# A long-convolution kernel with generated taps: decay tables laid out four channels wide, the input spectrum formed unfolded on TensorE, a new load order, evacuations on either engine

## The chip, the cores and the metric

One core of one Trainium2 chip. The metric is the device time of the whole kernel in microseconds (us), the median of four runs of each kernel. Each run also has a span (first to last instruction in the trace) and a mean granted TensorE clock; the time is about 2 us longer than the span. A run is called "fast" unless it is over 1.5% above the fastest of the same kernel. Engines: PE is TensorE, PEld its weight loads, DVE is VectorE, ACT is ScalarE, SP issues transfers.

## The reference, cut to what matters

```python
# x: [1, 2048, 512] bf16
dt = exp(log_dt); logdA = dt * (A_re + i A_im); dB = dt * (B_re + i B_im)
P  = exp(logdA[:, :, None] * l[None, None, :])          # 512 channels x 128 states x 2048 lags
K  = einsum("dn,dnl,dn->dl", C, P, dB).real             # the taps of a long convolution
y  = irfft(rfft(pad(u)) * rfft(pad(K)))[:, :, :L] + u * Dskip
# besides: a router picks 2 of 2048 rows, a small FFN (512 -> 1792 -> 512) updates them,
# and the result is g * y + (1 - g) * b, with g = sigmoid((x * gate_w).sum(-1))
```

The kernel never forms `P`. A lag is split into a sum of one of 32 coarse offsets and one of 21 others; each factor is a complex exponential, built in a table on ACT (exponentials and sines) and DVE (complex products). (The 32 x 21 = 672 sums are enough because the reference rounds the lags to bf16, so far fewer than 2048 of them differ.) Matmuls multiply the two tables over the 128 states and so form all taps: **tap generation**. One pair of matmuls (real and imaginary part) does a group of four channels, so a half takes 64 x 2 = 128; each multiplies 4 x 32 weights by 4 x 21 = 84 columns, and only the blocks in which both channels are the same are used. The 512 channels are done as two halves, "half 0" and "half 1". The convolution runs in the frequency domain with DFT matrices: **forward** (spectrum of the input), **kernel spectrum**, products on DVE, **inverse**. Each of these has two output blocks of 1024 steps.

## The kernel before: the parts that matter

Tables are stored one offset after another, each with its 256 channels in a row. Tap generation takes channels `g`, `g` + 64, `g` + 128 and `g` + 192 together, so both of its operands are strided. The weights (`TP`) lie 64 x 2 bytes = 128 bytes from element to element; in the moving operand (`TQ`) it is 256 x 2 = 512 bytes from one offset to the next.

```python
# tap generation: 128 matmuls of 84 columns for each half
for g in range(b0, b0 + ng):
    for part in range(2):
        last = hh.matmul(pb(0, 128, (g - b0) * 84, (1, 84)),
                         TP[h](0, 128, part * 32 * HC + g, (64, 128)),              # weights
                         TQ[h](0, 128, part * NJ * HC + g, (64, 4), (HC, NJ)),      # moving
                         start=(part == 0), stop=(part == 1))
# ... cut ...
# forward: even and odd steps apart (144 matmuls of 512 columns), ACT evacuates, DVE adds and subtracts
AC(ev(0, 128, 0, (1, 1024)), pb(0, 128, 0, (1, 1024)), ACTF.Copy, [pb.buf], [ev])
for pm in range(2):
    TT(o, i0, i1, SUB if pm else ADD, [ev], [...])
# ... cut ...
# the order of the work as it is handed to a list scheduler: exps1/tab1 and exps2/tab2 are exponentials and products
# of the two tables, xupd the update of rows by the FFN, kgen tap generation, kspec the kernel spectrum
exps1(0, 0); tab1(0, 1, False); routing(); forward()
exps2(0, 2); tab2(0, 3, False); exps1(1, 4); xupd(); tab1(1, 5, True); kgen(0)
exps2(1, 6); tab2(1, 7, True); kspec(0); kgen(1)
products(0, 0); products(0, 1); kspec(1); inverse(0); products(1, 0); products(1, 1); inverse(1)
```

All loads are issued by SP on one queue. A scheduler in the program places each operation by estimated costs when the kernel is built; on the chip every engine runs its list in that order and waits on semaphores.

## Time and profile before

| | before |
|---|---|
| time, median (range) | 292.08 us (291.55 to 294.74) |
| span of the profiled run | 291.4 us |
| PE, DVE, ACT busy | 191.5, 194.2, 143.4 us |
| tables done, first product may start (T) | 201.2 us |
| from T to the end | 90.2 us |

The first part of the page (busy time, share of the span, instruction count) and two rows of its second part (tenths in 40 slices of 7.3 us; PEclk is the granted clock):

```profile
PE 191.5 (66%) x1298; PEld 126.6 (43%) x1298; DVE 194.2 (67%) x347; ACT 143.4 (49%) x252; POOL 0.2 (0%) x4
...
DVE  0001796699799998110059619999991099999993
...
PEclk9999956959758655575555555589855579997999
```

No engine is full. DVE has three holes: before 27 us, near 130 to 148 us, and at 220 to 233 us. The groups (operation, count, busy us, mean ns, idle time before and what ended it):

```profile
L694 PE MATMUL ps<-AR 128*128 128x84 bf16 x256 | 47.9, 371 | 14.9 <-DVE AR L374 14.9
L694 PEld LDWEIGHTS ps<-AR 128*128 128x128 bf16 x256 | 45.0, 180 | 17.6 <-DVE AR L374 15.0
...
L735 PEld LDWEIGHTS ps<-AR 128*128 128x128 bf16 x224 | 22.0, 101 | 12.9 <-issue 2.9
```

L694 is tap generation. Its weight loads take 180 ns against 101 ns for a contiguous 128 x 128 load. The mean of one matmul there (371 ns) is a latency; what counts is how many finish in a stretch. The timeline of PE (start, us, operation, count, idle time before) gives that, and the timeline of DVE gives the holes:

```profile
108.99 13.43 PE L694 MATMUL ps<-AR 128*128 128x84 bf16 x72 [14.94 <-DVE AR L374]
...
205.80 23.73 PE L694 MATMUL ps<-AR 128*128 128x84 bf16 x128
229.35 2.65 PE L735 MATMUL ps<-AR 128*128 128x256 bf16 x8
```

```profile
27.18 0.69 DVE L374 TENSOR_TENSOR AR<-AR 128x512 f32<-128x512 bf16 x1 [27.18 <-ACT AR L385]
...
148.57 0.43 DVE L378 TENSOR_SCALAR AR<-AR 128x1024 bf16<-128x1024 bf16 x1 [19.41 <-ACT AR L385]
...
233.17 30.25 DVE L374 TENSOR_TENSOR AR<-AR 128x2048 bf16<-128x2048 bf16 x33 [13.23 <-ACT AR L385]
```

From the first start of the 128 tap matmuls to the start of the next matmul it is 229.35 - 205.80 = 23.55 us, 184 ns each. All rates below are taken in this way, as the duration of a row holds its last matmul's latency too. (The prediction names T as 200.6 and has 186 ns; the last table operation begins at 200.5 and ends at 201.2.) The hole of 13.23 us at 220 to 233 stands behind that stretch: the kernel spectrum that the products need is queued on PE after it.

### The profile page before, as it was taken

The page shows a single profiled execution, that of the slowest core. Times are in us where ns is not written, and L with a number is a line of the kernel's source. Part 1 is how long each engine was busy: PE and PEld are TensorE (multiplying, and loading weights), DVE is VectorE, ACT ScalarE, POOL GpSimd, SP SyncE. Part 2 cuts the span into 40 slices and gives each one's busy share as a digit, 9 for nine tenths or more (in the row PEclk, how much of TensorE's full clock was granted, in tenths as well). Part 3 has the DMA queues.
Part 4 walks back from the last instruction along what each step waited for, and adds up shares of the span by engine and source line. Part 5 has one row for each costly group of instructions (what it writes and reads, how often), then busy time and mean ns, then how long its engine had stood idle before and what let it go on. Part 6 is the DMA issues. An engine that isn't in the chain of part 4 may idle for free.

```text
span 291.4 us, 3307 instructions
## 1 busy us (share of the span) xinstructions
PE 191.5 (66%) x1298; PEld 126.6 (43%) x1298; DVE 194.2 (67%) x347; ACT 143.4 (49%) x252; POOL 0.2 (0%) x4
## 2 busy tenths in 40 slices
PE   0089109839319009999820250999999989977994
PEld 0035003513304009758310100266899666665883
DVE  0001796699799998110059619999991099999993
ACT  1023058997992402425999989855422335410000
POOL 0000000000000000000000000000000000000000
PEclk9999956959758655575555555589855579997999
DMA  7998690000160000000740000000000340002213
GB/s 283 351 207 127 183 369 1 3 0 0 43 208 2 0 0 1 2 0 0 291 213 0 3 0 0 0 0 2 0 0 2 103 184 2 1 0 74 58 52 108
DMA packets 21793, 20.97 MB, mean 72 GB/s; under 512 B 13073, under 2 KB 19346, under 8 KB 21394
## 3 DMA queue, kind: packets, MB, share of 16 engines
q1 hardware_dynamic: 21778, 20.76, 23.1%
q8 instruction: 10, 0.16, 0.2%
q14 instruction: 5, 0.04, 0.0%
HBM read 15.78 MB, written 2.10 MB: 61 GB/s over the span
## 4 chain that ended last, share of the span: by engine, by line
DVE 38%; PE 32%; ACT 16%; SPq 9%; issue 3%; DMA 1%; DVEq 0%
DVE AR L374 29%; PE ps L694 15%; ACT AR L385 14%; PE ps L735 6%; DVE AR L381 6%; SPq L448 6%; DVE AR L378 3%; PE ps L785 2%; PE ps L652 2%; PE ps L669 2%; PE ps L803 2%; PE ps L802 2%; ACT L231 2%; SPq L388 1%; DMA AR<-in_A_B_re_dram 1%
## 5 line engine op out<-in xcount | busy, mean ns | idle before, releaser
L374 DVE TENSOR_TENSOR AR<-AR 128x1024 bf16<-128x1024 bf16 (+6 forms) x222 | 146.6, 728 | 59.5 <-ACT AR L385 56.0
L385 ACT ACTIVATE AR<-AR 128x256 bf16<-128x256 f32 (+5 forms) x164 | 75.1, 542 | 31.7 <-DVE AR L374 11.5
L385 ACT ACTIVATE AR<-ps 128x1024 bf16<-128x1024 f32 (+6 forms) x64 | 50.7, 806 | 78.3 <-PE ps L694 31.0
L669 PE MATMUL ps<-AR 128*128 128x512 bf16 x128 | 37.9, 443 | 31.2 <-ACT AR L385 17.1
L694 PE MATMUL ps<-AR 128*128 128x84 bf16 x256 | 47.9, 371 | 14.9 <-DVE AR L374 14.9
L694 PEld LDWEIGHTS ps<-AR 128*128 128x128 bf16 x256 | 45.0, 180 | 17.6 <-DVE AR L374 15.0
L669 PEld LDWEIGHTS ps<-AR 128*128 128x128 bf16 x128 | 13.8, 112 | 50.5 <-ACT AR L385 18.4
L735 PE MATMUL ps<-AR 128*128 128x256 bf16 x224 | 34.0, 289 | 0.7 <-ACT AR L385 0.7
L785 PE MATMUL ps<-AR 128*128 128x256 bf16 x256 | 30.2, 281 | 4.4 <-DVE AR L381 4.4
L785 PEld LDWEIGHTS ps<-AR 128*128 128x128 bf16 x256 | 25.5, 101 | 8.8 <-DVE AR L381 5.0
L735 PEld LDWEIGHTS ps<-AR 128*128 128x128 bf16 x224 | 22.0, 101 | 12.9 <-issue 2.9
L378 DVE TENSOR_SCALAR AR<-AR 128x256 int32<-128x256 f32 (+5 forms) x48 | 12.7, 327 | 21.8 <-ACT AR L385 21.6
L381 DVE SCALAR_TENSOR_TENSOR AR<-AR 128x1024 int16<-128x1024 int16 (+2 forms) x20 | 22.8, 1148 | 0.1
L802 PE MATMUL ps<-AR 128*128 128x512 bf16 x16 | 9.3, 578 | 17.1 <-ACT AR L385 17.1
L707 PE MATMUL ps<-AR 128*32 128x128 bf16 (+1 forms) x96 | 8.6, 379 | 13.2 <-ACT AR L385 13.2
L381 DVE SCALAR_TENSOR_TENSOR AR<-ps,AR 128x256 bf16<-128x256 f32 x32 | 13.1, 475 | 2.4 <-PE ps L785 2.4
L802 PEld LDWEIGHTS ps<-AR 128*128 128x128 bf16 x16 | 1.7, 105 | 22.5 <-ACT AR L385 20.5
L385 ACT ACTIVATE AR<-ps,AR 128x512 bf16<-128x512 f32 x16 | 10.2, 682 | 1.8 <-PE ps L803 1.8
L707 PEld LDWEIGHTS ps<-AR 128*32 128x32 bf16 x96 | 3.9, 122 | 16.3 <-ACT AR L385 14.6
L803 PE MATMUL ps<-AR 2*128 2x512 bf16 x16 | 9.2, 575 | 0.0
L599 PE MATMUL ps<-AR 128*128 128x128 f32 x4 | 1.5, 374 | 10.8 <-DVE AR L378 10.8
L672 PE MATMUL ps<-AR 128*128 128x512 bf16 x16 | 7.1, 443 | 0.0
(29 smaller groups left out, 48.2 us busy)
## 6 DMA issues: line engine op xcount, KB each, us to landing
AR<-c_ksp SPq DMA_DIRECT2D x1, 3584.0 KB, 11.1
AR<-c_fwd SPq DMA_DIRECT2D x1, 2048.0 KB, 7.6
AR<-in_A_u_dram SPq DMA_DIRECT2D x2, 1024.0 KB, 11.0
AR<-c_inv SPq DMA_DIRECT2D x1, 2048.0 KB, 7.8
out_dram<-AR SPq DMA_DIRECT2D x16, 128.0 KB, 2.2
AR<-in_B_w_gate_dram SPq DMA_DIRECT2D x1, 1792.0 KB, 7.3
AR<-in_B_w_up_dram SPq DMA_DIRECT2D x1, 1792.0 KB, 11.3
AR<-in_B_w_down_dram SPq DMA_DIRECT2D x1, 1792.0 KB, 7.4
```

Source lines behind the costliest of these rows:

```text
L374: return P.op(DVE, lambda h: h.tensor_tensor(out=o, in0=a, in1=b, op=op), rd, wr, cost=tt_cost(o, a, b), **k)
L378: return P.op(DVE, lambda h: h.tensor_scalar(out=o, in0=a, scalar1=s1, scalar2=None, op0=op0), rd, wr, cost=c, **k)
L381: return P.op(DVE, lambda h: h.scalar_tensor_tensor(out=o, in0=a, scalar=sc, in1=b, op0=op0, op1=op1), rd, wr, cost=0.16 + nel(o) * 1.04e- ...
L385: return P.op(ACT, lambda h: h.activation(out=o, in_=a, func=func, scale=scale, bias=bias), rd, wr, cost=0.185 + nel(o) * 0.833e-3 + (0.09 ...
L448: P.op(SP, lambda h, db=db: h.dma_start_transpose(XT(0, 128, db * L, (1, L)), dr(A_u, db * 128, (D, L), (1, 128))), [], [(XT, db)], cost=0 ...
L669: last = h.matmul(pb(0, 128, par * 512, (1, 512)), F(0, 128, ((par * 4 + st) * 2 + part) * 512 + ft * 128, (1, 128)), U(0, 128, (blk * 8 + ...
L694: last = hh.matmul(pb(0, 128, (g - b0) * 84, (1, 84)), TP[h](0, 128, part * 32 * HC + g, (64, 128)), TQ[h](0, 128, part * NJ * HC + g, (64 ...
L707: last = hh.matmul(pb(32 * g, 32, c4 * 64, (256, njg), (1, 64)), lw, KA[h](0, 128, c4 * NJ + 8 * bk + g, (4, njg), (84, 64)), start=True, ...
L735: last = hh.matmul(pb(0, 128, n * 256, (1, 256)), KP(0, np_, u * 2048 + tau * 128, (1, 128)), KC[h](0, np_, jg * 256, (1, 256)), start=(k ...
L785: last = hh.matmul(pb(0, 128, e * 256, (1, 256)), G(0, 128, ((par * 2 + part) * 4 + ft) * 512 + (2 * t2 + e) * 128, (1, 128)), X(0, 128, h ...
L802: h.matmul(pb(0, 128, c0, (1, D)), IDN(0, (1, 128)), U(0, 128, tb * D, (1, D)), start=True, stop=False)
L803: return h.matmul(pb(0, 128, c0, (1, D)), OHR(0, 2, tb * 128, (1, 128)), ZB(0, 2, D, (1, D)), start=False, stop=True)
```

## The change

The intent: make both operands of tap generation contiguous, take additions from DVE, start the tables earlier, and let evacuations go to whichever of ACT and DVE the scheduler finds free first. Tables get the layout (64 groups of channels) x (offset) x (4 channels), so for one group the 128 weights lie in a row, and so do the 84 moving columns. ACT and DVE then write and read in runs of four bf16 values.

```diff
-   TP[h](0, 128, part * 32 * HC + g, (64, 128)),  TQ[h](0, 128, part * NJ * HC + g, (64, 4), (HC, NJ))
+   TP[h][1 - part](0, 128, g * 128, (1, 128)),    TQ[h][1 - part](0, 128, g * 84, (1, 84))
 # exponentials, an example
-   AC(TP[h](0, 128, 32 * HC + s * HC, (1, HC)), AL(0, 128, h * HC, (1, HC)), ACTF.Exp, ...)
+   AC(TP[h][1](0, 128, s * 4, (128, 64), (1, 4)), AL(0, 128, h * HC, (4, 64), (1, 4)), ACTF.Exp, ...)
 # cosine: an addition to the integer argument in place of an absolute value
-   STT(hv(1), hv(0), -1.0, hv(0), ALU.mult, ALU.max, ks, [(a, "abs")])
+   TS(w, w, 16384.0, ALU.add, ks, ks)
 # forward: sum and difference formed in PSUM, with a negated matrix: 272 matmuls, no DVE additions
-   AC(ev(...), pb(...), ACTF.Copy, [pb.buf], [ev]);  TT(o, i0, i1, SUB if pm else ADD, [ev], ...)
+   w = ng(...) if par and pm else F(...);  EV(X(...), pb(...), [pb.buf], ...)
 # copies out of PSUM and scalings: either engine, chosen when the schedule is made
+   def EV(o, a, rd, wr, **k): return P.op((ACT, DVE), (activation Copy, tensor_copy), rd, wr, ...)
 # loads: decay parameters first on SP; input U, DFT matrix F and small constants on ACT's queue
-   for i in range(6): P.op(SP, ... dma_start_transpose(PRM ...) ...)
+   for i in (1, 0, 2, 3, 4, 5): P.op(SP, ... dma_start_transpose(PRM ...), prio=...)
+   DMA([(U ...)], ..., eng=ACT, prio=2e5);  DMA([(F ...)], ..., eng=ACT, prio=1.9e5)
 # the last stage of half 0: ACT scales the inverse into YA, DVE adds it (16 updates leave DVE)
+   AC(YA(...), pb(...), ACTF.Copy, ..., scale=SG(...));  TT(u, u, YA(...), ADD, ...)
 # order
-   exps1(0, 0); tab1(0, 1, False); routing(); forward(); exps2(0, 2); tab2(0, 3, False); ...
+   exps1(0, 0); exps2(0, 0); routing()  # boosted;  tab1(0, (1, 1)); forward(); tab2(0, (1, 3)); ...
```

The diff also regroups ACT's loads of function tables (8 loads of 1.28 us in the trace of before) and changes some of the scheduler's estimated costs.

## The prediction

> **What bounds it now.** Span 291.4 us. Busy line: DVE 194 us, PE 192, ACT 143; none is full. Chain of waits: DVE 38%, PE 32%, ACT 16%. Stretches, by the timeline:
> 1. DVE starts at 27 us: the parameter transposes are issued behind the input, its transposes and the DFT matrix.
> 2. Tables of half 0 on DVE, to 120.
> 3. First tap generation (L694): 72 matmuls in 13.4 us, 186 ns each. DVE idles 129 to 148 us, waiting for ACT's exponentials (19.4 in the waits).
> 4. Tables of half 1, to T = 200.6 us.
> 5. Products and inverse, T to the end: 91 us, of which DVE waits 13.2 us (220 to 233) for the kernel spectrum stuck behind the second tap generation (128 matmuls, 23.7 us).
>
> **What the change does.**
> - Tap weights are contiguous. Their loads now take 180 ns (groups by form). Contiguous loads with 2-column matmuls ran 64 in 1.74 us, 27 ns each; 84 columns warm are about 35 ns (512 took 215). Estimate: 50 to 90 ns per matmul, 128 in 8 to 11 us instead of 23.7. The Trainium skill (SBUF — State Buffer, 16-byte cachelines) says that each access crossing to a new line pays; weights 128 bytes apart do. Runs of four bf16 should keep DVE's rate (1024 elements 0.70 us); that is my main doubt.
> - Forward: 32 DVE adds of 0.43 us vanish (-13.8), but PE goes from 144 to 272 matmuls of 512 columns: 58 us warm (215 ns), against 31. Cold they take 427 ns (both rates are in this trace).
> - 16 absolute values (1.38 us each) become integer adds (about 0.7, from 0.43 for 512 fp32 elements): -11 us DVE. Some scalings and 16 output updates leave DVE; a few evacuations join. DVE total about 165 us; ACT about 155; PE 170 to 190.
> - DMA: decay parameters first on one queue, input and matrix on the other. ACT starts its 48 exponentials (0.32 us each) near 8 us, DVE tables near 26, without the pause of stretch 3.
> - In the instruction order, routing and its FFN now precede the forward transform on PE. Weights land about 33 us; I expect the forward to start at 40 to 46 us instead of 14.
>
> **Critical path after.** Forward plus first tap generation occupy PE about 75 us (58 + 10 + cold start and some FFN), to 116 to 121. The second half's exponentials reuse memory of the negated matrices and wait for it, about 9 us of ACT, then tab2 of half 1, about 33 us on DVE: T = 155 to 162. After T, 91 - 13.2 = 78 us remain, since tap generation now hides behind the first products (15 us). Sum: 235 us. The PE doubling is on the path and eats part of the gain.
>
> **Predicted: 235 us**, 8 in 10 between 218 and 252. Faster over 2%: 0.97; within 2%: 0.02; slower: 0.01.
>
> **What would show it.** L713 at 90 ns or less per matmul; DVE busy 160 to 172; DVE tables starting before 30 us; forward starting at 40 to 46; T near 158; no wait over 3 us between T and the last products; 1024-element DVE products still 0.70 us.
>
> **What would make it wrong.** Four-wide runs slow DVE or ACT (1.2 us per 1024-element product would add about 40 us); in-order EV copies on DVE or ACT stall tables behind a late forward (slower); routing finishing early or evacuations overlapping better, T near 140 (faster, about 218).

## The result, and the profile after

| | before | after |
|---|---|---|
| time, median (range) | 292.08 (291.55 to 294.74) | 246.94 (244.86 to 248.39) us |
| ratio | 1 | 0.843, 95% interval 0.835 to 0.852 |
| PE, DVE, ACT busy | 191.5, 194.2, 143.4 | 172.5, 170.4, 146.9 us |
| T | 201.2 | 162.7 us |
| from T to the end | 90.2 | 82.0 us |

A ratio here is the mean time of one kernel's fast runs over the mean of the other's fast runs in the same rounds, so it is not quite the ratio of the medians quoted beside it.

The change is 45 us faster, within the predicted range, and 12 us short of the number predicted. The same rows of the page and the same groups as before:

```profile
PE 172.5 (70%) x1426; PEld 103.4 (42%) x1426; DVE 170.4 (70%) x279; ACT 146.9 (60%) x278; POOL 0.2 (0%) x4
...
DVE  0002223899995039989850299969999999999872
...
PEclk9999999999999999999999755589997999996798
...
L713 PE MATMUL ps<-AR 128*128 128x84 bf16 x256 | 11.8, 201 | 2.4 <-ACT AR L402 2.4
L713 PEld LDWEIGHTS ps<-AR 128*128 128x128 bf16 x256 | 10.6, 98 | 4.5 <-ACT AR L402 3.2
```

Weight loads of tap generation went from 180 to 98 ns. The timeline of PE shows the first tap matmuls, the start of the forward and the end of the kernel:

```profile
59.33 10.18 PE L693 MATMUL ps<-AR 128*128 128x512 bf16 x40
...
111.41 1.07 PE L713 MATMUL ps<-AR 128*128 128x84 bf16 x24
112.31 3.61 PE L693 MATMUL ps<-AR 128*128 128x512 bf16 x16
...
204.59 14.15 PE L804 MATMUL ps<-AR 128*128 128x256 bf16 x128
224.27 16.64 PE L804 MATMUL ps<-AR 128*128 128x256 bf16 x128 [5.53 <-ACT AR L398]
```

24 tap matmuls took 112.31 - 111.41 = 0.90 us from the first start to the next matmul's, 37.5 ns each, about a fifth of before. But the forward (L693) began at 59.3 us, and 128 inverse matmuls (L804) start only when the last product of block 1 is done (224.8 us); they run on for 11.2 us after the last product of all (229.7). The start of the kernel, on the timelines of DVE and ACT, and the landing times of transfers (last number, us from issue):

```profile
22.62 0.69 DVE L387 TENSOR_TENSOR AR<-AR 128x512 f32<-128x512 bf16 x1 [10.30 <-DMA AR<-in_A_A_im_dram]
...
41.28 0.69 DVE L391 TENSOR_SCALAR AR<-AR 128x1024 int32<-128x1024 int32 x1 [3.62 <-ACT AR L398]
...
89.59 1.23 DVE L402 CAST AR<-ps 128x1024 bf16<-128x1024 f32 x1 [12.81 <-PE ps L695]
```

```profile
24.99 0.72 ACT L406 ACTIVATE AR<-AR 128x256 int32<-128x256 f32 x2 [10.70 <-DVE AR L387]
...
26.54 12.34 ACT L398 ACTIVATE AR<-AR 128x256 bf16<-128x256 f32 x40
```

```profile
AR<-in_A_A_re_dram SPq DMA_TRANSPOSE x1, 10.3
AR<-in_A_A_im_dram SPq DMA_TRANSPOSE x1, 19.4
```

The two decay parameters were issued first, yet `A_im` landed 19.4 us after its issue; before, its transpose took 3.9 us. `A_im` is needed for the argument scalings (L406), which ACT has in its list ahead of 40 of the exponentials. Those exponentials need only `A_re`, but ACT runs its list in order and the scalings stand first, so they ran at 26.5 to 38.9 us and the tables on DVE started at 41.3.

### The profile page after: what moved, and what is told of

Its sections match the earlier page's. It is cut to its first block, busy times and chain, and to the rows that moved or that the text cites. A ratio compares the mean times of both kernels' runs of the same rounds, so it can differ in the third digit from the quotient of the medians.

```text
span 244.7 us, 3534 instructions
## 1 busy us (share of the span) xinstructions
PE 172.5 (70%) x1426; PEld 103.4 (42%) x1426; DVE 170.4 (70%) x279; ACT 146.9 (60%) x278; POOL 0.2 (0%) x4
## 4 chain that ended last, share of the span: by engine, by line
PE 43%; DVE 24%; ACT 20%; DMA 8%; issue 3%; SPq 1%; DVEq 0%; ACTq 0%
DVE AR L387 21%; PE ps L693 19%; ACT AR L398 13%; DMA AR<-in_A_A_im_dram 8%; PE ps L804 7%; PE ps L754 6%; ACT AR L402 3%; PE ps L831 3%; PE ps L830 2%; ACT AR L406 2%; DVE AR L391 2%; PE ps L659 1%; PE ps L670 1%; PE ps L695 1%; ACT L242 1%
## 5 line engine op out<-in xcount | busy, mean ns | idle before, releaser
L387 DVE TENSOR_TENSOR AR<-AR 128x1024 bf16<-128x1024 bf16 (+5 forms) x182 | 136.8, 804 | 34.7 <-DMA AR<-in_A_A_re_dram 11.6
L398 ACT ACTIVATE AR<-AR 128x256 bf16<-128x256 f32 (+2 forms) x132 | 64.7, 560 | 15.4 <-DVE AR L391 4.8
L402 ACT ACTIVATE AR<-ps 128x1024 bf16<-128x1024 f32 (+6 forms) x58 | 45.5, 806 | 30.7 <-PE ps L754 17.7
L693 PE MATMUL ps<-AR 128*128 128x512 bf16 x256 | 59.6, 385 | 0.0
L693 PEld LDWEIGHTS ps<-AR 128*128 128x128 bf16 x256 | 25.1, 99 | 30.5 <-issue 1.9
L804 PE MATMUL ps<-AR 128*128 128x256 bf16 x256 | 30.8, 286 | 5.5 <-ACT AR L398 5.5
L804 PEld LDWEIGHTS ps<-AR 128*128 128x128 bf16 x256 | 26.1, 103 | 10.0 <-DVE AR L387 5.8
L754 PEld LDWEIGHTS ps<-AR 128*128 128x128 bf16 x224 | 21.9, 101 | 12.2 <-issue 1.5
L398 ACT ACTIVATE AR<-ps,AR 128x512 bf16<-128x512 f32 (+1 forms) x32 | 16.6, 586 | 15.5 <-DVE AR L387 10.4
L598 PE MATMUL ps<-AR 128*128 128x2 bf16 x64 | 1.8, 165 | 32.2 <-DMA AR<-in_A_u_dram 32.2
L406 ACT ACTIVATE AR<-AR 128x256 int32<-128x256 f32 x50 | 17.6, 405 | 10.9 <-DVE AR L387 10.7
L391 DVE TENSOR_SCALAR AR<-AR 128x1024 int32<-128x1024 int32 (+5 forms) x32 | 16.2, 524 | 8.4 <-ACT AR L398 8.0
L402 DVE CAST AR<-ps 128x1024 bf16<-128x1024 f32 (+3 forms) x6 | 5.1, 865 | 22.5 <-PE ps L695 15.4
L830 PE MATMUL ps<-AR 128*128 128x512 bf16 x16 | 8.1, 509 | 11.0 <-ACT AR L398 11.0
L598 PEld LDWEIGHTS ps<-AR 128*128 128x128 bf16 x64 | 1.8, 104 | 32.1 <-issue 32.1
L713 PE MATMUL ps<-AR 128*128 128x84 bf16 x256 | 11.8, 201 | 2.4 <-ACT AR L402 2.4
L713 PEld LDWEIGHTS ps<-AR 128*128 128x128 bf16 x256 | 10.6, 98 | 4.5 <-ACT AR L402 3.2
L617 PE MATMUL ps<-AR 128*128 128x128 f32 x4 | 1.9, 475 | 12.8 <-DVE AR L391 12.8
L394 DVE SCALAR_TENSOR_TENSOR AR<-ps,AR 128x256 bf16<-128x256 f32 x16 | 6.9, 479 | 4.1 <-PE ps L804 4.1
L830 PEld LDWEIGHTS ps<-AR 128*128 128x128 bf16 x16 | 1.6, 100 | 15.7 <-ACT AR L398 14.6
## 6 DMA issues: line engine op xcount, KB each, us to landing
AR<-in_B_w_up_dram SPq DMA_DIRECT2D x1, 1792.0 KB, 11.2
```

Of the source, the lines that this page charges most:

```text
L387: return P.op(DVE, lambda h: h.tensor_tensor(out=o, in0=a, in1=b, op=op), rd, wr, cost=tt_cost(o, a, b), **k)
L391: return P.op(DVE, lambda h: h.tensor_scalar(out=o, in0=a, scalar1=s1, scalar2=None, op0=op0), rd, wr, cost=c, **k)
L398: return P.op(ACT, lambda h: h.activation(out=o, in_=a, func=func, scale=scale, bias=bias), rd, wr, cost=0.185 + nel(o) * 0.833e-3 + (0.09 ...
L402: return P.op((ACT, DVE), (lambda h: h.activation(out=o, in_=a, func=ACTF.Copy), lambda h: h.tensor_copy(o, a)), rd, wr, cost=(0.185 + n * ...
L406: return P.op((ACT, DVE), (lambda h: h.activation(out=o, in_=a, func=ACTF.Copy, scale=c), lambda h: h.tensor_scalar(out=o, in0=a, scalar1= ...
L693: last = h.matmul(o, w, U(0, 128, (blk * 8 + st * 2 + par) * D, (1, D)), start=(par + st == 0), stop=(par * 4 + st == 7 and blk == 0))
```

## The experiments

Twelve kernels ran, each timed in three rounds beside the kernel before (medians of before: 292.2 to 292.9 us). Ratios are to before. "After" alone is 0.843.

| run | time, us (range) | ratio (95%) | result |
|---|---|---|---|
| second YA buffer | 246.87 (246.56 to 249.10) | 0.846 (0.842 to 0.850) | correct |
| half 0's updates back on DVE | 250.94 (250.47 to 251.57) | 0.858 (0.855 to 0.861) | correct |
| input and matrix held back | 238.41 to 249.11, two pairs | 0.816 (0.812 to 0.820), 2 fast runs | correct |
| one queue | 239.02 (237.76 to 240.06) | 0.816 (0.811 to 0.821) | correct |
| weights strided | 251.68 (248.99 to 253.78) | 0.856 (0.850 to 0.863) | see text |
| moving operand strided | 271.95 (268.50 to 272.44) | 0.926 (0.919 to 0.933) | wrong |
| both strided | 277.73, 1 fast run; others 282.1 to 284.4 | none given | wrong |
| folded, first try | 250.53 (248.90 to 250.66) | 0.854 (0.850 to 0.859) | wrong by mistake |
| evacuations on ACT alone | 248.40 (247.38 to 248.69) | 0.849 (0.844 to 0.853) | correct |
| before, parameters first | 287.83 (286.93 to 289.19) | 0.983 (0.976 to 0.990) | correct |
| one queue, products reordered | 236.32 (236.16 to 237.88) | 0.808 (0.803 to 0.813) | correct |
| one queue, folded | 233.99 (233.13 to 234.72) | 0.799 (0.794 to 0.804) | correct |

### What the layout is worth

My explanation in the prediction was the weights' strided load. If that is all, striding the weights alone brings the old tap generation back, and striding the moving operand does nothing. In these three runs the tables stay as in after; only addresses in the tap matmuls differ, so wrong values are multiplied, in the same number of instructions.

Weights alone:

```diff
-   TP[h][1 - part](0, 128, g * 128, (1, 128)),
+   TP[h][1 - part](0, 128, g, (64, 128)),
```

> The changed kernel, but the tap matmuls read their 128 weights 128 bytes apart, as before the change; the moving side stays contiguous. The result is wrong on purpose, the instructions and their order are the same. Theory A (the weight load was what cost 186 ns): 170 to 190 ns per tap matmul instead of 44, second tap generation 22 to 24 us instead of 8, total 15 to 30 us above the changed kernel, 260 to 275 us. Rival B (the strided moving side was the cost): 60 ns or less per matmul, total within 3 us of the changed kernel.

The moving operand alone:

```diff
-   TQ[h][1 - part](0, 128, g * 84, (1, 84)),
+   TQ[h][1 - part](0, 128, g, (64, 84)),
```

> The changed kernel, but the tap matmuls read their 84 moving columns 128 bytes apart, as before; weights contiguous. Wrong result on purpose, same instructions and order. Theory A (weights): below 80 ns per tap matmul, total within 4 us of the changed kernel. Rival B (moving side): 150 ns or more per matmul and total over 258 us.

Both edits together:

> The kernel after with both operands of the tap matmuls read 128 bytes apart, as the kernel before reads them; only the two addresses differ, the tables stay where they are, so the taps are wrong on purpose. It tells how much of the whole gain the contiguous layout carries, and whether the two operands' costs add. Theory A (they add): 44.5 + 47 + 101 = 193 ns for a matmul, 24 of them in 4.6 us and 128 in 24 to 25 us, close to the 185 ns of the kernel before; the time rises by 30 us or more over after (the two single runs rose by 4.8 and 25), to 276 to 284 us. Rival M (weight loads hide behind the slower matmuls, so that the larger of the two counts): 146 to 155 ns, 24 in 3.6 us, and 270 to 274 us as in the run with the moving operand alone.

The second tap generation on the timeline of PE, weights strided, then the moving operand strided, then both:

```profile
182.21 11.72 PE L713 MATMUL ps<-AR 128*128 128x84 bf16 x128
193.76 1.77 PE L754 MATMUL ps<-AR 128*128 128x256 bf16 x8
```

```profile
194.13 18.66 PE L713 MATMUL ps<-AR 128*128 128x84 bf16 x128
212.62 2.65 PE L754 MATMUL ps<-AR 128*128 128x256 bf16 x8
```

```profile
201.70 23.42 PE L713 MATMUL ps<-AR 128*128 128x84 bf16 x128
224.94 2.65 PE L754 MATMUL ps<-AR 128*128 128x256 bf16 x8
```

From the first start to the next matmul's, that is 90, 144 and 182 ns for a matmul, against 37.5 with neither and 184 in before. The theory that the weight load is the cause fell: it is the smaller part, +53 ns; the moving operand's stride costs +107 ns. Both single runs missed the figures written for them: 90 lies between the two theories, and 144 just under the rival's 150. The two costs nearly add: the sum for both would be 197 and 182 was measured, so the rival (the larger of the two counts, 144) fell too. My expectation for the last run has 44.5 + 47 + 101 = 193 instead; its 44.5 is 1.07 us by 24, the last matmul's latency included. A second correction to it: before reads its moving columns 512 bytes apart, not 128. The time per matmul is the same within 2 ns, so beyond 128 bytes the distance did not show.

An obvious rival is the granted clock, which was low in before's second tap generation. The traces rule it out for these times. Before's tap matmuls took 186 ns at a clock of 0.50, 185 at 0.83 and 184 at 0.58; with both strided it was 182 at 0.57 and at about 0.8, and with the moving operand strided 144 at 0.98 and at 0.54.

In whole-kernel time: weights alone +4.1 us by the fast runs (median 251.0; one of the four is labelled slow), moving alone +25.0, both +31 in the one fast run (277.73 against 246.94), 35 to 37.5 in the three runs labelled slow. These three were 1.6% to 2.4% above the fourth at the same clock of 0.86. So, taken out of after, the contiguous layout carries roughly 31 of the 45 us that the change brought; that size rests on one fast run. The other 14 were not parted: the integer additions, the earlier exponentials and the table loads were not run alone. Nor was the mean granted clock held fixed: it was 0.73 in before, 0.93 in after and 0.86 with both strided, so how much of the 31 us comes by way of the clock of other matmuls is not known. The check of results passed the run with strided weights although its addresses are wrong; the error of the other two was 0.024. Nothing in the argument rests on their values.

The stride of 128 bytes also has a page. The Trainium skill ("SBUF — State Buffer", Specifications) gives 16-byte cachelines and says that each cross to a new line pays a penalty. The runs agree in direction, and give the sizes that the page lacks. They do not show that the line of 16 bytes is the reason, as no stride between contiguous and 128 bytes was run.

### The new load order

One part of the change alone, put into the kernel before: the time steps and parameters are issued first, on its one queue.

```diff
-   ... [], [LDT], 131072)
+   ... [], [LDT], 131072, prio=2e5)
-   ... [], [(PRM, i)], cost=0.07, nbytes=131072)
+   ... [], [(PRM, i)], cost=0.07, nbytes=131072, prio=1.9e5 - 1e3 * i)
```

> The kernel before with one thing of the change alone: the time steps and the six decay and coefficient parameters are issued before the input, its transposes and the DFT matrix, on the one queue that it has. It separates the new DMA order from the rest. Theory O (order carries much of the gain): DVE starts at about 8 to 10 us instead of 27, and the 18 us come through wholly or half: 275 to 284 us (ratio 0.94 to 0.97). Rival P (the order alone is worth little, because the tables of half 0 then meet the forward's evacuations and adds and the exponentials of half 1 still sit behind ACT's other work): 288 to 293 us, ratio 0.985 or more, although DVE starts early. The transposes should land in 3 to 5 us each, as in the kernel before.

DVE started at 5.8 us instead of 27.2, and the time fell by 4.4 us (287.83 against 292.25), ratio 0.983. That is the rival's side, slightly under its range. Where the 21.4 us went can be read from the waits (engine and line, what it waited for: total us, times, longest). Before, then before with parameters first:

```profile
DVE AR L374 <- ACT AR L385: 56.0, 6, 27.2
...
DVE AR L378 <- ACT AR L385: 21.6, 2, 19.4
...
DVE AR L383 <- PE ps L652: 7.1, 1, 7.1
```

```profile
DVE AR L374 <- ACT AR L385: 40.6, 8, 12.9
...
DVE AR L383 <- PE ps L652: 18.6, 1, 18.6
...
DVE AR L378 <- ACT AR L385: 15.4, 2, 12.3
```

Of the 56.0 us in before, 27.2 are the start itself. Without it, the three waits changed by (40.6 - 28.8) + (18.6 - 7.1) + (15.4 - 21.6) = 17.1 us: an early DVE waits for ACT instead, and for the FFN's result (L652), which stands behind the slow tap generation on PE. 21.4 - 17.1 leaves the 4.3 us that the time shows.

In after, the disputed cost is `A_im`'s late landing. Theory: plain copies of 4 MB on ACT's queue share the DMA engines with the parameters' transposes. Hold back the copies of the input and of the matrix until `A_im` has landed:

```diff
 # loads of U and of F on ACT's queue
-   [], [(U, t) for t in ...], ...
+   [(PRM, 1)], [(U, t) for t in ...], ...
-   [], [F], ...
+   [(PRM, 1)], [F], ...
```

> The changed kernel, but the loads of the input and of the transform matrix on ScalarE's queue are issued only once the imaginary decay parameters have landed. Theory A (those parameters land at 22.6 us because 4 MB of plain copies on the other queue share the same DMA engines): they land before 8 us, ScalarE's exponentials run without the 10.7 us pause and end near 24 us instead of 38.9, forward transform starts at 48 to 52 us instead of 59 (the transposed input still lands near 32), total 236 to 242 us. Rival B (transposes are slow to land whatever else runs, or a later limit takes the gain back): parameters land after 15 us, or they land early but total stays within 2 us of the changed kernel.

`A_im` landed 4.6 us after its issue and DVE's first work came at 6.9 us, so that part held. The time did not follow in half of the runs: 248.37 and 249.11, labelled slow, then 238.41 and 238.66, all four at clocks of 0.93 to 0.94. The profiled run is a slow one. In it the four transposes of the input, on SP's queue, met the held-back copies instead (median to landing):

```profile
AR<-in_A_u_dram SPq DMA_TRANSPOSE x4, 16.1
```

Their median is 5.6 us in after, and PE's first work, which needs them, began at 38.3 us (32.2 in after). What differs in the fast pair is not known, as no fast run of this kernel was profiled, and a slow profile explains no time. The fast pair matters all the same: two queues are still in use there, and 0.816 is the ratio of the next run, which keeps one queue and chooses the order:

```diff
-   ... 1048576, eng=ACT, prio=2e5)      # U
+   ... 1048576, prio=1.05e5 - j)
-   ... 2097152, eng=ACT, prio=1.9e5)    # F
+   ... 2097152, prio=1.04e5)
 # the small constants likewise: the two gate vectors and CB move to SP
```

> The changed kernel with every load on one queue in the order of need: decay parameters, transposed input, the other parameters, then input, transform matrix and FFN weights. Theory A (queue sharing delays the transposed input too, and routing waits for it): transposed input lands near 18 us instead of 32, routing is then limited by FFN weights landing near 40 us, forward starts at 42 to 48 us, total 230 to 238 us. Rival B (the order of the bytes does not matter because VectorE and ScalarE limit from there on): total above 243 us.

All four runs are at 237.8 to 240.1 us, 8 us under after. `A_im` landed in 3.1 us, the exponentials ended at 21.9 instead of 38.9, DVE's tables began at 24.3 instead of 41.3 and the forward at 47.6 instead of 59.3:

```profile
AR<-in_A_A_im_dram SPq DMA_TRANSPOSE x1, 3.1
```

```profile
9.57 12.33 ACT L398 ACTIVATE AR<-AR 128x256 bf16<-128x256 f32 x40
```

```profile
24.30 0.69 DVE L391 TENSOR_SCALAR AR<-AR 128x1024 int32<-128x1024 int32 x1 [0.29 <-ACT AR L398]
```

```profile
45.71 1.65 PE L659 MATMUL ps<-AR 128*128 128x2 bf16 x56 [3.02 <-DMA AR<-in_B_w_up_dram]
47.61 9.26 PE L693 MATMUL ps<-AR 128*128 128x512 bf16 x31 [0.24 <-issue]
60.29 3.60 PE L693 MATMUL ps<-AR 128*128 128x512 bf16 x8 [3.42 <-ACT AR L402]
```

So plain copies in flight beside the early transposes cost about 8 us, and the late landing is shown as the larger part of the miss. That it is these copies, and not the second queue as such, rests on the fast pair above; and this run also changes the order of the other loads. The Trainium skill ("DMA: Bandwidth & Descriptors", Issuing engines are not separate DMA queues) says that transfers from scalar, sync and gpsimd run on the same 16 DMA engines and interleave, and that a second issuing engine saves only issue time. These runs agree: 19.4 us to landing beside another queue's copies, 3.1 on one queue ahead of them.

Yet only 7 of the 17 us by which the tables started earlier reached T (155.7 against 162.7). The rest is a wait of DVE:

```profile
125.38 1.23 DVE L402 CAST AR<-ps 128x1024 bf16<-128x1024 f32 x1 [17.00 <-PE ps L695]
```

The forward ended at 125.3 us (127.1 in after) although it began 12 us earlier; it had lost 3.4 us at an evacuation, and its first matmuls ran slowly (31 in 9.26 us, then 8 in 3.60, where later 8 take 1.89), and tap generation and FFN work lay between. Part of half 1's second set of exponentials lies in the memory of the negated matrices and so waits for that end.

### Does the forward's unfolding pay?

The prediction said that the doubled PE work is on the path. First try, on after: the folded forward of before (144 matmuls, additions on DVE).

```diff
 def forward():
-   for pm in range(2): ... w = ng(...) if par and pm else F(...) ...; EV(X(...), pb(...))
+   for part in range(2): ... 8 matmuls per part ...; EV(ev(...), pb(...)); TT(o, i0, i1, SUB if pm else ADD, ...)
```

> The changed kernel with the forward transform folded again (144 wide matmuls and 32 adds on VectorE in place of 272 matmuls), evacuations still on either engine. The scheduler then puts part of it ahead of routing. Theory A (TensorE's doubled forward is on the critical path, from its start to the first tap generation; VectorE has idle time of about 25 us there to take 13.8 us of adds): second half's tables end earlier, total 232 to 242 us, faster than the changed kernel. Rival B (VectorE is the limit all along, so unfolding was right): 8 to 15 us slower, 254 to 262 us.

The result was wrong, by my mistake: block 1's first evacuation overwrote the buffer that its second matmul group still had to read. The time, 250.53, was 3.6 us over after, and I took it as a sign that unfolding pays. The mistake also chains the second matmul group behind an evacuation, so this run is not a clean test. Second try, on the one-queue kernel, with both matmul groups of block 1 issued ahead of the evacuations:

> One-queue order as in the run at 239.0, with the forward transform folded again as in the kernel before (144 matmuls instead of 272, sums and differences on DVE, 32 more additions), this time with both matmul groups of block 1 issued ahead of the evacuations, so that the result should be right. It tells whether forming the spectrum unfolded on PE pays. Theory U (unfolding pays because DVE is the scarcer engine): PE ends the forward earlier by up to 25 us, but DVE gains 14 us of additions ahead of the tables of half 1: 241 to 248 us. Rival V (PE's 58 us of forward matmuls were on the path from the late start to the second exponentials, and unfolding costs time): 228 to 236 us. The earlier folded run, on the two queues and with a wrong result, was at 250.5 against 246.9, so U is favoured.

It is correct and at 233.99 us, 5.0 under the one-queue kernel, with intervals that do not overlap. Rival V was right, against what I favoured: folded is faster here. The edit brings two things with it. The scheduler now starts the forward ahead of the FFN, at 39.3 us instead of 47.6, and 1 MB of negated matrices is no longer loaded. So the 5.0 us belong to folding together with the order that follows from it.

```profile
39.30 4.55 PE L687 MATMUL ps<-AR 128*128 128x512 bf16 x16
```
Busy times, one queue unfolded, then one queue folded:

```profile
PE 176.6 (74%) x1417; PEld 104.4 (44%) x1426; DVE 169.7 (71%) x277; ACT 149.3 (63%) x280; POOL 0.2 (0%) x4
```

```profile
PE 154.4 (67%) x1298; PEld 93.2 (40%) x1298; DVE 180.7 (78%) x311; ACT 147.4 (64%) x278; POOL 0.2 (0%) x4
```

Folding adds 11 us to DVE and takes 22 from PE. The added DVE work went where DVE was waiting: between 24.3 us and T, DVE's idle time fell from 40.2 us (131.35 less 91.20 busy) to 24.2 us (126.00 less 101.81). The last forward matmul came at 114 us instead of 125, half 1's second exponentials ended at 125.8 instead of 130.3, and T fell from 155.7 to 150.3. From T to the end little changed (82.7 and 81.4 us). Why the first try on two queues came out slower stays open; its mistake and its late tables are both candidates, and no run parts them.

### The either-engine evacuations

DVE waited 12.81 us in after in front of an evacuation that the scheduler had given it. All such copies back on ACT:

```diff
 def EV(o, a, rd, wr, **k):
-   return P.op((ACT, DVE), ...)
+   return AC(o, a, ACTF.Copy, rd, wr, **k)
```

> The changed kernel with all plain evacuations on ScalarE only, as before the change. Theory A (the 12.8 us that VectorE waited for TensorE in front of one evacuation cost nothing, since the sines that its next work needs came from ScalarE only at 90 us): total within 3 us of the changed kernel, 244 to 250 us. Rival B (the in-order evacuation on VectorE stalls the tables): 6 to 12 us faster, below 241 us.

248.40 us, 1.5 over after, intervals overlapping. The wait was not removed but renamed: DVE now waited 13.98 us there for ACT's sines. The choice of engine is worth at most a little; what DVE waited for came late on either road.

### The end of the kernel

After T, 82.0 us passed where I had predicted 78. First suspect: the buffer `YA` is shared by the two output blocks, and ACT waits 10.4 us for it. A second buffer:

```diff
-   YA = B("ya", oI + 16 * KB, 4 * KB)
+   YA = [B("ya1", oI + 16 * KB, 4 * KB), B("ya0", oE, 4 * KB)]
```

> The changed kernel with a second buffer for the scaled inverse of the second block of half 0, nothing else. Theory A (the tail lost about 10 us because ScalarE could not write the second block's scaled rows until VectorE had added the first block's, which stands late in VectorE's order, so PSUM stayed full and TensorE stood still from about 219 to 224 us): the 10.4 us wait of ScalarE on VectorE goes, the inverse of half 1 starts on TensorE during the last products, from the last product to the end takes 12 to 14 us instead of 21, total 236 to 240 us. Rival B (the tail is long because the last products or the last updates on VectorE are late by themselves): total within 2 us of the changed kernel, 245 to 249 us.

The long wait disappeared and the time did not move (246.87 against 246.94). In this run, too, 128 inverse matmuls start after the last product of block 1 and fill the end (block 0's last products run beside their first 5 us):

```profile
226.65 15.63 PE L804 MATMUL ps<-AR 128*128 128x256 bf16 x128 [4.48 <-DVE AR L387]
```

Second suspect: moving half 0's 16 updates from DVE to ACT bought nothing here. Undo it:

```diff
-   if h == 0:
+   if False:
```

> The changed kernel with the output update of half 0 put back on VectorE as scalar_tensor_tensor from PSUM, as before the change. Theory A: moving it to ScalarE cost more in the tail than it saved; VectorE does 16 more updates of about 0.42 us less 4 adds of 0.66 us, so about +4 us of work, but the tail falls to 12 to 14 us: total 240 to 244 us, faster than the changed kernel although VectorE has more to do. Rival B (VectorE's work is what counts in the last stage): 4 us slower than the changed kernel, 250 us or more.

250.94 us, 4.0 over after. The removed DVE work counts: 16 updates of about 0.43 us came back and 4 additions of about 0.66 us left, 4.2 us by that sum. So both DVE's work and then PE's row of 128 matmuls are on the path in this stage. If that is right, ordering half 1's products by block lets PE do block 1's 64 matmuls while DVE forms block 0:

```diff
-   products(1, 0);  products(1, 1)
+   products(1, 0, (1,));  products(1, 1, (1,));  products(1, 0, (0,));  products(1, 1, (0,))
```

> The kernel after with all loads on one queue in order of need (239.0 us as a run) and, besides, the products of half 1 ordered by output block: block 1 of both quarters first, then block 0 of both, so that the 64 inverse matmuls of block 1 can run while DVE forms block 0. Theory (the end is a row of PE work that waits for the last block 1 product): after the last product only 64 matmuls are left, 8.3 us instead of 16.8, and the time falls by 3 to 6 us, to 233 to 236 us (ratio to before 0.795 to 0.805). Rival (DVE's own work is the limit in this stretch: the 16 output updates only move from after the products to between them): within 2 us of 239.

236.32 us, 2.7 under the one-queue kernel; the two intervals overlap narrowly (0.803 to 0.813, 0.811 to 0.821). The row is split as meant:

```profile
215.34 7.16 PE L804 MATMUL ps<-AR 128*128 128x256 bf16 x64 [2.87 <-ACT AR L398]
223.31 7.16 PE L804 MATMUL ps<-AR 128*128 128x256 bf16 x64 [0.81 <-DVE AR L394]
```

The gain is just under the expected 3 to 6 us. DVE's last product ended 0.6 us earlier (222.5 against 223.1 us), and 8 output updates then stood ahead of the last 64 matmuls' results. About 1 us of the gain lies before T (154.5 against 155.7). The fastest kernel that ran is the folded one-queue kernel at 233.99 us, 20% under before. This reordering on top of it was not run.

## Why the prediction was right or wrong

- **Faster by over 2%, and the range: right.** 246.94 lies in 218 to 252. The number 235 was 12 us too low. It was a sum of span stretches, and the time is about 2 us longer than the span, which I left out.
- **Tap generation at 50 to 90 ns: right in size and better, 37.5.** The reason was wrong. "Weights 128 bytes apart do [pay]" explains 53 of the 147 ns; the moving operand's stride, which I did not mention, costs 107.
- **The 128 matmuls "hide behind the first products": right.** The 13.2 us wait after T became 2.1 us.
- **Four-wide runs keep DVE's and ACT's rates: right.** The 1024-element product took 687 ns. This was my main doubt.
- **Integer additions at about 0.7 us: right, 689 ns. DVE about 165 us: 170.4, in the range named; PE 172.5 in 170 to 190; ACT 146.9 instead of 155.**
- **"Decay parameters first on one queue, input and matrix on the other", exponentials near 8 us, tables near 26: wrong.** This is the step that failed. I took the parameters' landing times from a trace in which they had one queue. Beside the other queue, `A_im` took 19.4 us. The exponentials ended at 38.9 and tables began at 41.3 us.
- **"I expect the forward to start at 40 to 46 us": wrong, 59.3.** It is the consequence. With one queue it started at 47.6, still late because the FFN's weights landed at 45.7 and its matmuls stand ahead of the forward.
- **"Forward plus first tap generation occupy PE about 75 us": right in size, 59.3 to 130, 71 us.**
- **Table of half 1 "about 33 us on DVE": mis-sized.** It ran from 140.6 to 162.7, 22 us. That hid most of the late start: T came out at 162.7, just past 155 to 162.
- **"After T, 78 us remain": mis-sized, 82.0.** I had taken 91 less the lost wait and not looked at what ends last: in before the last 64 inverse matmuls ended 8.0 us after the last product, in after the row of 128 ended 11.2 us after it.
- **"The PE doubling is on the path and eats part of the gain": right.** Undone on one queue, together with the order that the scheduler then makes, 5.0 us come back.
- **"In-order EV copies on DVE or ACT stall tables behind a late forward": seen, and not binding.** The wait of 12.8 us is there, but giving all copies to ACT gained nothing.

## What to carry to other kernels

For a stream of short matmuls, look at the strides of both operands: here the moving side's cost twice the weights', and the two nearly added. Ask of every early load which other transfers will be in flight beside it, and do not carry a landing time from a trace with one queue to a program with two. Before moving work from a busy engine to another, ask where the busy engine waits: here 11 us of DVE work that fell into its waits came with 22 us less on PE and a gain of 5.0 us, while 4 us of DVE work put into the last stage, where DVE was waited for, cost 4.0.

## What the Trainium skill lacked or had wrong

- "SBUF — State Buffer" (Specifications, cachelines) gives a penalty for each new line without a size or the operand it falls on. For an 84-column bf16 matmul with 128 weights: 37.5 ns contiguous, 90 with the weights 128 bytes apart, 144 with the moving operand so, 182 with both.
- The same page (Who interferes with whom) calls PE's read ports for the moving operand and for LDWEIGHTS independent. In a stream of short matmuls their strides' costs still nearly added: 182 ns measured, 197 by the sum, 144 if only the larger counted.
- "TensorE: Matmul & The Clock Gate" (Back-to-back issue gap) has 81 ns per matmul with its load at 128 columns as a sustained figure, and a formula that gives an estimate of 37.5 ns at 84 columns for the isolated gap. The page says that the formula counts too little for pairs of load and matmul at few columns, yet contiguous pairs of load and 84-column matmul ran at 37.5 ns here, as the formula has it. It gives no time for strided weights, whose loads took 180 ns in the kernel before, or for a strided moving operand.
- "DMA: Bandwidth & Descriptors" says that a transpose next to ordinary DMAs needs nothing (Rules for kernel authors). That is about safety. In time, a 128 KB transpose went from 3.1 us to landing to 19.4 beside 4 MB of plain copies on the other queue, and no section gives such a size.
- No page has the two kinds of execution seen with the held-back copies: 238.4 and 238.7 us, or 248.4 and 249.1, on one core, all at clocks of 0.93 to 0.94.
